# Moving one batch's chunk loads and two FFT insertions by a few steps in a filter-then-FFN kernel

## The chip, the cores and the metric

The kernel runs on one core of one Trainium2 chip. The metric is device time in microseconds (us). One execution can also be profiled; the profile is a page of summaries and a trace of all instructions. TensorE is PE in its lines, its weight loads PEld, VectorE DVE, ScalarE ACT, GpSimd POOL, and the queue of DMA issues on SyncE SPq.

## The reference

A spectral filter along the sequence, then a gated feed-forward network (FFN):

```python
X = np.fft.rfft(x, axis=1)                    # x: 8 x 3008 x 256, float32
y = np.fft.irfft(X * (filt_r + 1j*filt_i), n=3008, axis=1)
t = y.reshape(24064, 256)
out = (np.maximum(t @ w_gate, 0) * (t @ w_val)) @ w_out    # d_ff = 1536
```

## The kernel before

The FFN is the main loop: 47 blocks of 512 tokens, 12 steps each, so 564 steps. Step number n is block n // 12, ft n % 12. The FFT of later batches is cut in pieces that the loop puts between steps through a table of callbacks, `side`. Names used below: **psV, psG, psO** are the PSUM tiles of the FFN; **psF** is that of an excursion ("tiled A", the first DFT stage of a quarter batch); **dC** is a filtered spectrum read back from memory (Dbuf), which **psY** turns into **yT**, the FFN's input; **XP** is a chunk of x.

```python
def load_chunk(b, j):                 # six transfers, issued by GpSimd
    ...
def fold_chunk(b, j):                 # six adds on GpSimd, t from a pool of 2
    t = fs.tile([128, 2, 512], FP32, tag="fold", bufs=2, name="fold")
    tt(t, xp[:, 0:2], xp[:, 2:4], op=ALU.add)
    ...                               # cut: five more
def tiled_a(b, j):                    # the excursion
    banks = [ps.tile([128, 2, D], FP32, tag=t, name="psF") for t in ("psv", "psg", "fft", "fft")]
    ...                               # cut: 32 matmuls, then copies to asb (two on ScalarE, two on VectorE)

def hold_gpsimd(tile_):               # a tiny copy: GpSimd goes on when tile_ is written
    scr = sb.tile([128, 8], FP32, tag="scr", bufs=2)
    nc.gpsimd.tensor_copy(scr[:tile_.shape[0]], tile_)
...
C_AT = (8, 10)                        # the steps of a block at which psY is made (halves 0 and 1)
for b in range(1, B):
    end = (b * S // W - 1) * NFT + C_AT[0] - 5          # 123 for batch 2
    ...
        for j, e in enumerate((-74, -69, -64, -57)):
            l = (22, 34, 34, 46)[j] if b == 2 else end - 113 + NFT * j
            def next_x(b=b, j=j, l=l):
                hold_gpsimd(yTs[l // NFT + 1][:, 0, 0:8])
                load_chunk(b, j)
                if j: fold_chunk(b, j - 1)
                if j == 3: fold_chunk(b, j)
            at_step(l, next_x)
            at_step(end + e, lambda b=b, j=j: tiled_a(b, j))
...
for k in range(NB):
    for ft in range(NFT):
        gv(k, ft, prods)                                # psV, psG; ScalarE copies psV, VectorE makes prod
        if prev is not None: o_part(prev[0], ft, prev[1])   # four psO
        for f in side.get(k * NFT + ft, ()): f()        # FFT pieces
        if ft in C_AT and k + 1 < NB: item_c(k + 1, C_AT.index(ft))   # psY, then the copy to yT
```

Of the kernel before, what the change touches and what calls it, by code (L numbers as in the profile page):

```python
# [120 lines left out]
def kernel(  # L121
# [13 lines left out]
    NFT = DFF // 128  # L135
# [119 lines left out]
    def hold_gpsimd(tile_):  # L255

        scr = sb.tile([128, 8], FP32, tag="scr", bufs=2)
        nc.gpsimd.tensor_copy(scr[:tile_.shape[0]], tile_)  # L258
# [32 lines left out]
    def load_chunk(b, j):  # L291

        xp = XP[j]
        for q in range(4):
            r, o = 32 * q, 8 * q + 2 * j
            nc.gpsimd.dma_start(xp[r:r + 24, 0:4:2, :],  # L296
                              _ap(x, (b * N1 * N2 + o) * D,
                                  [[N2 * D, 24], [47 * N2 * D, 2], [1, 512]]))
        for i in range(2):
            nc.gpsimd.dma_start(xp[:, 2 * i + 1, :],  # L300
                              _ap(x, ((b * N1 + 46 + 47 * i) * N2 + 2 * j) * D,
                                  [[8 * D, 4], [-N2 * D, 32], [1, 512]]))

    def fold_chunk(b, j):

        xp = XP[j]
        t = fs.tile([128, 2, 512], FP32, tag="fold", bufs=2, name="fold")
        tt = nc.gpsimd.tensor_tensor
        tt(t, xp[:, 0:2], xp[:, 2:4], op=ALU.add)  # L309
        tt(xp[:, 2:4], xp[:, 0:2], xp[:, 2:4], op=ALU.subtract)  # L310
        tt(xp[:, 0], t[:, 0], t[:, 1], op=ALU.add)
        tt(t[:, 0], t[:, 0], t[:, 1], op=ALU.subtract)
        tt(t[:, 1], xp[:, 2], xp[:, 3], op=ALU.add)
        tt(xp[:, 2], xp[:, 2], xp[:, 3], op=ALU.subtract)
        fold[b, j] = (xp[:, 0], t[:, 0], t[:, 1], xp[:, 2])

    def tiled_a(b, j):

        banks = [ps.tile([128, 2, D], FP32, tag=t, name="psF") for t in ("psv", "psg", "fft", "fft")]
        for c in range(4):  # L320
            for q in range(4):
                r = 32 * q
                nc.tensor.matmul(banks[q][32 * c:32 * c + 32], WF[r:r + 24, c, :],  # L323
                                 fold[b, j][c][r:r + 24], start=True, stop=True,
                                 tile_position=(r, 32 * c))
        asf = sb.tile([128, NC2 * D], BF16, tag="asb", bufs=4, name="asb")
        asf = asf.rearrange("p (n q d) -> p n q d", n=2, d=D)
        for q in range(4):
            copy = nc.scalar.copy if q % 2 == 0 else nc.vector.tensor_copy
            copy(asf[:, :, q, :], banks[q])  # L330
        for c in range(4):
            nc.sync.dma_start(_ap(Abuf[b], ((48 * (c % 2) + 24 * (1 - c // 2)) * N2 + 8 * j) * D,
                                  [[N2 * D, 24], [1, 8 * D]]),
                              asf[32 * c:32 * c + 24])

    def load_at_tiled(b):

        ats[b] = sb.tile([128, NG, D], BF16, tag="at", bufs=1, name="at")
        for rr in range(4):
            nc.sync.dma_start(ats[b][32 * rr:32 * rr + 32],  # L340
                              _ap(Abuf[b], (48 * (rr % 2) + 24 * (rr // 2)) * N2 * D,
                                  [[D, 32], [N2 * D, 24], [1, D]]))
# [4 lines left out]
    def load_at(b, c):  # L347
        if c == 0:
            ats[b] = sb.tile([128, NG, D], BF16, tag="at", bufs=1, name="at")
        nc.sync.dma_start(ats[b][c:c + 125:4],  # L350
                          _ap(Abuf[b], c * NROW * NC2 * D, [[D, 32], [4 * NC2 * D, NG], [1, D]]))
# [4 lines left out]
    def fwd(b, i):  # L356

        for e in range(2):
            psXs[b, i, e] = ps.tile([128, 2, D], FP32, tag=fft_tag(), name="psX")
        for m in range(2):  # L360
            for e in range(2):
                for a in range(2):
                    j = 12 * a + 2 * i + m
                    nc.tensor.matmul(psXs[b, i, e][64 * a:64 * a + 64, m],  # L364
                                     F2[64 * e:64 * e + 64, j, :],
                                     ats[b][64 * e:64 * e + 64, j, :], start=True, stop=True,
                                     tile_position=(64 * e, 64 * a))

    def product(b, i, e, k, pool=False):

        psX = psXs[b, i, e]
        pool_, bufs = (fs, 4) if b else (pro, 6)
        p = pool_.tile([128, 2, D], BF16, tag=("tt", "uu")[k], bufs=bufs, name=("tt", "uu")[k])
        filt = (Ftr, Fti)[k][:, 4 * i + e:4 * i + 4:2, :]
        if pool:
            xs = pro.tile([128, 2, D], FP32, tag="xs", bufs=3)
            nc.scalar.copy(xs, psX)
            nc.gpsimd.tensor_tensor(p, xs, filt, op=ALU.mult)
        else:
            nc.vector.tensor_tensor(p, psX, filt, op=ALU.mult)  # L380
        tus[b, i, e, k] = p

    def inv(b, i, tags=None, cuts=CUTS):

        if i in cuts:
            dsbs[b] = i, sb.tile([128, 2, 4, D], BF16, tag="dsb", bufs=3, name="dsb")
        i0, dsb = dsbs[b]
        psD = [ps.tile([128, 2, D], FP32, tag=tags[a] if tags else fft_tag(), name="psD")
               for a in range(2)]
        for m in range(2):  # L390
            for k in range(2):
                for a in range(2):
                    for e in range(2):
                        nc.tensor.matmul(psD[a][64 * e:64 * e + 64, m],  # L394
                                         (I2t, I2u)[k][64 * a:64 * a + 64, 4 * i + 2 * m + e, :],
                                         tus[b, i, e, k][64 * a:64 * a + 64, m],
                                         start=(k == 0), stop=(k == 1),
                                         tile_position=(64 * a, 64 * e))
        o = 2 * (i - i0)
        for a in range(2):  # L400
            nc.scalar.copy(dsb[:, a, o:o + 2, :], psD[a])  # L401
        if i + 1 in cuts:
            nc.sync.dma_start(_ap(Dbuf[b], 2 * i0 * D, [[NG * D, 128], [NG // 2 * D, 2], [1, (o + 2) * D]]),
                              dsb[:, :, :o + 2, :])
# [18 lines left out]
    def load_d(b, z0=0, z1=NZ):  # L423
        for z in range(z0, z1):
            dC = sb.tile([NROW, 8, D], BF16, tag="dC", bufs=6)
            for e in range(2):
                nc.sync.dma_start(dC[48 * e:48 * e + 48],
                                  _ap(Dbuf[b], (64 * e + 16 * z) * NG * D,
                                      [[D, 48], [48 * D, 8], [1, D]]))
            dCs[b, z] = dC  # L430

    yTs = {}
# [177 lines left out]
    def at_step(s, f):  # L610
        side.setdefault(s, []).append(f)
# [5 lines left out]
    for b in range(1, B):  # L617
        end = (b * S // W - 1) * NFT + C_AT[0] - 5
        if b == 1:
            for c in range(2, 4):  # L620
                at_step(c - 2, lambda c=c: load_at(1, c))
        else:
            for j, e in enumerate((-74, -69, -64, -57)):
                l = (22, 34, 34, 46)[j] if b == 2 else end - 113 + NFT * j

                def next_x(b=b, j=j, l=l):
                    hold_gpsimd(yTs[l // NFT + 1][:, 0, 0:8])
                    load_chunk(b, j)
                    if j:
                        fold_chunk(b, j - 1)  # L630
                    if j == 3:
                        fold_chunk(b, j)
                at_step(l, next_x)
                at_step(end + e, lambda b=b, j=j: tiled_a(b, j))
            at_step(end + e + 4, lambda b=b: load_at_tiled(b))
        for i in range(7):
            l = -35 + 5 * i if b == 1 else -40 + 6 * i
            if i < 6:
                at_step(end + l, lambda b=b, i=i: fwd(b, i))
                for h in range(4):  # L640
                    at_step(end + l + h, lambda b=b, i=i, h=h: product(b, i, h // 2, h % 2))
            if i > 0:
                at_step(end + l, lambda b=b, i=i: inv(b, i - 1, ("psv", "psg")))
        at_step(end - 2, lambda b=b: load_d(b))
    prev = None
    for k in range(NB):
        prods = []
# [39 lines left out]
```

## Time and profile before

| | before |
|---|---|
| three runs known at the prediction | 899.38, 900.00, 900.28 us |
| the profiled run | 897.68 us, span 895.6 us |
| TensorE busy | 871.2 us, 97% |
| VectorE, ScalarE, GpSimd | 64%, 56%, 41% |
| mean granted clock | 0.999 |

TensorE is the bound, so a change pays by what it takes out of TensorE's own gaps. The prediction shows the gaps in batch 2. One more gap, in batch 5, in the timeline of TensorE (columns: start, duration, engine, line, operation, tiles, form, count; in brackets the idle time before and its releaser):

```profile
572.56 0.27 PE L451 MATMUL psY<-M,dC 96*128 96x4 bf16 x3
573.72 0.30 PE L451 MATMUL psY<-M,dC 96*128 96x94 bf16 x4 [0.89 <-DMA dC<-Dbuf]
```

The seven psY matmuls, normally in one go, are split: four waited for the data of dC.

### The profile page before, as it was taken

To read this page: it belongs to the slowest core of one execution; us is meant where nothing else is said; L and a number is where in the kernel's file an instruction comes from. 1 tells how busy PE (TensorE), PEld (TensorE's weight loads), DVE (VectorE), ACT (ScalarE), POOL (GpSimd) and SP (SyncE) were. 2 spreads that over 40 slices of the span, in tenths; PEclk is the share of its full clock that TensorE was granted. 3 is DMA by queue.
4 is the path that set the end of the run, shared out by engine and by line. 5 is a ranking of instruction groups with operands and counts; after the bars stand their busy time and mean duration, and the time that the engine had idled before them with its cause. 6 is when DMAs were issued, how large, how long until landed. Compare 5 with 4: busy or idle time off the path is not lost.

```text
span 895.6 us, 19081 instructions
## 1 busy us (share of the span) xinstructions
PE 871.2 (97%) x7086; PEld 507.4 (57%) x7206; DVE 569.3 (64%) x873; ACT 499.3 (56%) x891; POOL 364.4 (41%) x361
## 2 busy tenths in 40 slices
PE   7899999999999999999999999999999999999997
PEld 2335555566556665556655566556655556666665
DVE  2736865577665776667766676657766577655553
ACT  3475565556555556555655556555565555655553
POOL 4351399138661386415682167801868000000001
PEclk9999999999999999999999999999999999999999
DMA  8998358534466435563375333762346512231111
GB/s 240 284 241 166 110 143 181 123 81 113 128 156 132 112 106 133 136 141 95 100 174 135 97 99 106 180 134 85 110 143 150 119 31 82 74 81 36 37 32 52
DMA packets 114098, 109.17 MB, mean 122 GB/s; under 512 B 20359, under 2 KB 98599, under 8 KB 113366
## 3 DMA queue, kind: packets, MB, share of 16 engines
q1 hardware_dynamic: 90294, 80.10, 34.6%
q0 software_dynamic: 22992, 26.41, 12.4%
q8 instruction: 56, 0.92, 0.5%
q10 hardware_dynamic: 720, 1.45, 0.5%
q14 instruction: 36, 0.29, 0.1%
HBM read 61.93 MB, written 49.81 MB: 125 GB/s over the span
## 4 chain that ended last, share of the span: by engine, by line
PE 75%; POOL 6%; issue 5%; DVE 4%; DMA 4%; ACT 4%; SPq 0%; POOLq 0%; DVEq 0%; ACTq 0%
PE psG L467 23%; PE psO L486 22%; PE psV L467 21%; DVE prod L472 4%; ACT vsb L470 3%; PE psF L323 2%; PE psD L394 2%; PE psX L364 1%; DMA XP<-in_x_dram 1%; DMA Ftr<-in_filt_r_dram 1%; PE psY L451 1%; POOL XP L296 1%; DMA dC<-Dbuf 1%; POOL fold L309 1%; POOL XP L310 1%
## 5 line engine op out<-in xcount | busy, mean ns | idle before, releaser
L472 DVE SCALAR_TENSOR_TENSOR prod<-psG,vsb 128x512 bf16<-128x512 f32 x564 | 389.2, 690 | 263.5 <-ACT vsb L470 257.3
L470 ACT CAST vsb<-psV 128x512 bf16<-128x512 f32 x564 | 332.1, 589 | 261.3 <-PE psV L467 160.2
L486 PE MATMUL psO<-WoT,prod 128*128 128x256 bf16 x2256 | 336.4, 273 | 1.1
L467 PE MATMUL psG<-yT,WgT 128*128 128x512 bf16 x1107 | 330.8, 379 | 6.7 <-ACT dsb L401 0.6
L467 PE MATMUL psV<-yT,WvT 128*128 128x512 bf16 x1030 | 315.2, 380 | 0.3 <-ACT vsb L470 0.3
L486 PEld LDWEIGHTS <-prod 128*128 128x128 bf16 x2256 | 220.6, 98 | 143.4
L467 PEld LDWEIGHTS <-WgT 128*128 128x128 bf16 x1128 | 110.0, 98 | 135.8 <-issue 2.4
L467 PEld LDWEIGHTS <-WvT 128*128 128x128 bf16 x1128 | 98.4, 98 | 42.0 <-issue 30.8
L258 POOL CAST scr<-yT 128x8 f32<-128x8 bf16 x25 | 4.7, 189 | 262.2 <-ACT yT L456 262.2
L509 POOL DMA_DIRECT2D out_dram<-osb x5 | 2.6, 536 | 195.9 <-ACT osb L499 195.9
L380 DVE TENSOR_TENSOR tt<-psX,Ftr 128x512 bf16<-128x512 f32 x96 | 65.1, 683 | 7.1 <-PE psX L364 7.1
L499 ACT COPY osb<-psO 128x512 f32<-128x512 f32 x92 | 53.9, 586 | 27.4 <-PE psO L486 25.4
L309 POOL TENSOR_TENSOR fold<-XP 128x1024 f32<-128x1024 f32 x24 | 56.5, 2355 | 19.8 <-PE psF L323 19.6
L380 DVE TENSOR_TENSOR uu<-psX,Fti 128x512 bf16<-128x512 f32 x89 | 60.6, 681 | 0.0
L401 ACT CAST dsb<-psD 128x512 bf16<-128x512 f32 x96 | 51.5, 589 | 12.1 <-PE psD L394 11.7
L296 POOL DMA_DIRECT2D XP<-in_x_dram x96 | 56.7, 596 | 3.2 <-PE psG L467 1.6
L310 POOL TENSOR_TENSOR XP<-XP 128x1024 f32<-128x1024 f32 x24 | 56.3, 2348 | 1.9
L330 DVE CAST asb<-psF 128x512 bf16<-128x512 f32 x48 | 30.9, 686 | 20.9 <-PE psF L323 20.9
L330 ACT CAST asb<-psF 128x512 bf16<-128x512 f32 x48 | 25.8, 589 | 32.0 <-PE psF L323 32.0
L456 ACT CAST yT<-psY 128x512 bf16<-128x512 f32 x47 | 27.5, 586 | 26.0 <-PE psY L451 25.2
L451 PE MATMUL psY<-M,dC 96*128 96x94 bf16 (+18 forms) x604 | 37.7, 198 | 1.5 <-DMA dC<-Dbuf 1.4
L458 DVE CAST yT<-psY 128x512 bf16<-128x512 f32 x47 | 32.0, 681 | 9.8 <-PE psY L451 9.8
(69 smaller groups left out, 492.5 us busy)
## 6 DMA issues: line engine op xcount, KB each, us to landing
at<-Abuf SPq DMA_DIRECT2D x32, 384.0 KB
dC<-Dbuf SPq DMA_DIRECT2D x64, 192.0 KB
XP<-in_x_dram POOLq DMA_DIRECT2D x48, 256.0 KB, 6.1
Dbuf<-dsb SPq DMA_DIRECT2D x23, 512.0 KB
XP<-in_x_dram POOLq DMA_DIRECT2D x96, 96.0 KB, 2.6
Abuf<-asb SPq DMA_DIRECT2D x96, 96.0 KB
out_dram<-osb SPq DMA_DIRECT2D x69, 94.0 KB
XF<-in_x_dram SPq DMA_DIRECT2D x15, 256.0 KB
```

Source lines behind the costliest of these rows:

```text
L296: nc.gpsimd.dma_start(xp[r:r + 24, 0:4:2, :], _ap(x, (b * N1 * N2 + o) * D, [[N2 * D, 24], [47 * N2 * D, 2], [1, 512]]))
L309: tt(t, xp[:, 0:2], xp[:, 2:4], op=ALU.add)
L310: tt(xp[:, 2:4], xp[:, 0:2], xp[:, 2:4], op=ALU.subtract)
L330: copy(asf[:, :, q, :], banks[q])
L380: nc.vector.tensor_tensor(p, psX, filt, op=ALU.mult)
L401: nc.scalar.copy(dsb[:, a, o:o + 2, :], psD[a])
L451: nc.tensor.matmul(psY[:, o:o + w], dCs[b, n2 // 8][:, n2 % 8, h * 128:(h + 1) * 128], M1[:, n1:n1 + w], start=True, stop=True)
L467: nc.tensor.matmul(pt[:, :W], w[:, h, ft * 128:(ft + 1) * 128], yt[:, h, :], start=(h == 0), stop=(h == 1))
L470: nc.scalar.copy(vsb, psV[:, :W])
L472: nc.vector.scalar_tensor_tensor(prod, in0=psG[:, :W], scalar=0.0, in1=vsb, op0=ALU.max, op1=ALU.mult)
L486: nc.tensor.matmul(psO[:, t % 2], prods[ft][:, t * 128:(t + 1) * 128], WoT[:, ft, :], start=(ft == 0), stop=(ft == NFT - 1))
L499: copy(osb[:, t0 % 2:t % 2 + 1], psO[:, t0 % 2:t % 2 + 1])
```

## The change

Its intent: GpSimd finished folding two chunks of batch 2 after TensorE wanted them. So in batch 2 the second and the fourth chunk's loads get an earlier step, and the last two excursions a step two later. In batches 3 to 8 all loads get a step two earlier. In all of them the hold ahead of a load is put on the product of the step itself rather than on the next block's yT.

```diff
-            for j, e in enumerate((-74, -69, -64, -57)):
-                l = (22, 34, 34, 46)[j] if b == 2 else end - 113 + NFT * j
+            for j, e in enumerate((-74, -69, -62, -55) if b == 2 else (-74, -69, -64, -57)):
+                l = (22, 29, 34, 43)[j] if b == 2 else end - 115 + NFT * j
                 def next_x(b=b, j=j, l=l):
-                    hold_gpsimd(yTs[l // NFT + 1][:, 0, 0:8])
+                    hold_gpsimd(prods[-1][:, 0:8])
```

## The prediction

> **What bounds the kernel now.** The first table of the page gives TensorE 871.2 us busy of a span of 895.6 us, 97%; VectorE has 64%, ScalarE 56%, GpSimd 41%. The chain that ended last is 75% TensorE. So only what stops TensorE can be worth anything, and the question is where it stops.
>
> The main loop has 47 blocks of 12 steps, 564 in all. One step is two psV matmuls, two psG, then four psO; a batch's FFT work is put between steps. A "tiled A excursion" (psF, 32 matmuls) is such an insertion: it reads a chunk of x that GpSimd has loaded and folded with six additions. I read the timeline of TensorE next, by the starts. A bare step runs from one psV to the next in 1.30 us (153.18, 154.48, 155.78). In batch 2 the loop puts the four excursions at steps 49, 54, 59 and 66 (end is 123; minus 74, 69, 64, 57), which are the psF starts at 130.99, 138.66, 146.83 and 158.47:
>
> ```profile
> 137.27 0.59 PE L467 MATMUL psV<-yT,WvT 128*128 128x512 bf16 x2
> ...
> 138.66 0.63 PE L323 MATMUL psF<-XP,WF 24*32 24x512 f32 x4
> ...
> 139.74 0.39 PE L467 MATMUL psV<-yT,WvT 128*128 128x512 bf16 x1
> ...
> 145.41 0.60 PE L467 MATMUL psV<-yT,WvT 128*128 128x512 bf16 x2
> ...
> 146.83 0.63 PE L323 MATMUL psF<-XP,WF 24*32 24x512 f32 x4
> ...
> 148.28 1.06 PE L323 MATMUL psF<-XP,WF 24*32 24x512 f32 x8 [0.29 <-POOL XP L314]
> 149.27 0.39 PE L467 MATMUL psV<-yT,WvT 128*128 128x512 bf16 x1
> ...
> 157.08 0.59 PE L467 MATMUL psV<-yT,WvT 128*128 128x512 bf16 x2
> ...
> 159.89 1.06 PE L323 MATMUL psF<-XP,WF 24*32 24x512 f32 x8 [0.28 <-POOL XP L314]
> 160.88 0.60 PE L467 MATMUL psV<-yT,WvT 128*128 128x512 bf16 x2
> ```
>
> The reader is to measure psV to psV across each. The second excursion takes 139.74 - 137.27 = 2.47 us, so a ready excursion costs 2.47 - 1.30 = 1.17. The third takes 149.27 - 145.41 = 3.86 and the fourth 160.88 - 157.08 = 3.80. They lose **1.39 and 1.33 us, 2.72 us together**. The bracket says only 0.29 and 0.28, because modelled ends of earlier matmuls cover most of the gap. The releaser is GpSimd's last fold addition, so I read its timeline:
>
> ```profile
> 105.67 0.19 POOL L258 CAST scr<-yT 128x8 f32<-128x8 bf16 x1 [15.01 <-ACT yT L456]
> ...
> 120.10 0.19 POOL L258 CAST scr<-yT 128x8 f32<-128x8 bf16 x1
> ...
> 134.13 0.19 POOL L258 CAST scr<-yT 128x8 f32<-128x8 bf16 x1
> ...
> 146.95 1.27 POOL L314 TENSOR_TENSOR XP<-XP 128x512 f32<-128x512 f32 x1
> 149.68 2.35 POOL L309 TENSOR_TENSOR fold<-XP 128x1024 f32<-128x1024 f32 x1 [1.46 <-PE psF L323]
> ...
> 158.57 1.27 POOL L314 TENSOR_TENSOR XP<-XP 128x512 f32<-128x512 f32 x1
> ```
>
> GpSimd sat idle until 105.67 (the hold on y) and was then busy without a gap until 148.2: the third fold ends there, after its excursion has begun, and the fourth ends at 159.84. The page names psF for the 1.46 us before 149.68, but the fold buffer needed there had been free since the second excursion (139.7). The chain of waits shows instead "137.32 12.12 DMA XP<-in_x_dram", that is, the fourth chunk landed at 149.44. So the queue started too late, and the last chunk landed late. In batch 3 all four excursions take 2.46 or 2.47 us: no other batch has anything to win here.
>
> **What the Trainium skill says.** "Perfetto Trace Analysis", section "Per-engine timelines", has a matmul's recorded end computed, not observed. The trace agrees: records of one step add to 0.59 + 0.59 + 0.60 = 1.78 us where starts are 1.30 apart. Hence I use starts. "GPSIMD Engine Reference", section 3.1, has a 2048-element fp32 add at 4497 ns; half of that is 2249, and the 1024-element adds here take 2355, so a fold is not shortened by moving it. "SBUF — State Buffer", section "Who interferes with whom", lets GpSimd and VectorE collide only where VectorE uses the shared ports, not with a single SBUF input. The product has one (the other is in PSUM), and it takes 0.69 us both at 150.95 beside a fold and at 165.10 with GpSimd idle: folds may move freely beside it. "DMA: Bandwidth & Descriptors", section "Issuing engines are not separate DMA queues", says that all transfers interleave on the same 16 engines; the 12.12 us of the fourth chunk beside the batch's dC load agree (the median landing over all XP issues is 2.7).
>
> **The change part by part.** No instruction is added or removed (the order of the two programs has the same rows on every engine). Three things move.
>
> *1. Batch 2's chunks.* Loads at steps 22, 34, 34, 46 become 22, 29, 34, 43, and the hold is on the product of that very step. Before, the holds were on y of the next block, made at ft 8, so steps 20, 32, 32, 44 set them free. From the trace: six load issues take 3.8 us (120.2 to 124.0), one fold 10.1 (124.0 to 134.1). Step 29's psV is near 98.4 (psV 103.23 is step 32, 2.18 before it step 31, two steps of 1.30 before that), its product ends near 100.4. Then GpSimd goes: loads 100.6 to 104.5, fold 1 to 114.6, loads to 118.5, fold 2 to 128.6, loads to 132.5, fold 3 (its buffer comes free with the first excursion, 132.3) to 142.5, fold 4 to 152.6. These are estimates from those durations: 5.6 us sooner for fold 3. If the fourth chunk again takes 12 us it lands near 144.5 and fold 4 ends near 154.6.
>
> *2. Two excursions two steps later.* The third moves to step 61, at 146.83 + 2 x 1.30 = 149.4, some 7 us after its fold. The fourth moves to 68, at 158.47 - 1.39 + 2.60 = 159.7, 5 to 7 us after its fold. Both waits go: **-2.72 us**. Either movement alone would nearly do (5.6 us sooner, or 2.6 later against 1.4 needed).
>
> *3. A new neighbour.* Step 68 is ft 8, where the next y is made straight after the excursion, with psY in the same pair of psv buffers. psV of step 68, psF, psY and psV of step 69 take turns in two buffers, so psV of step 69 must wait for ScalarE's copy of psF. At ft 1, 6 and 11 there is no psY and that copy is hidden. The copy starts 1.30 us after psF (132.29 against 130.99) and takes 0.59, and psV can start at about 1.94; without the wait it would at 1.07 + 0.27 (psY at 163.50, psV at 163.76) = 1.34. **+0.60 us.** There is a precedent in batch 1, an inverse transform followed by psY in one step:
>
> ```profile
> 126.24 0.41 PE L451 MATMUL psY<-M,dC 96*128 96x20 bf16 x7
> 126.50 0.38 PE L467 MATMUL psV<-yT,WvT 128*128 128x512 bf16 x1
> 127.43 0.59 PE L467 MATMUL psG<-yT,WgT 128*128 128x512 bf16 x2 [0.56 <-ACT dsb L401]
> ```
>
> *4. Batches 3 to 8.* Loads go from ft 10 to ft 8, but the old hold was already set free by ScalarE's y at ft 8: at 180.75 in batch 3, where the product of the same step ends at 180.27 (179.57 + 0.70). So they start only about 0.45 us sooner, and their folds 3 and 4 still wait for psF. The one loss there is in batch 5, where dC arrived late (a wait of 0.9 us at 573.7, after a Dbuf write that shared the DMA engines with a chunk). It may shrink: I put -0.1.
>
> Sum: -2.72 + 0.60 - 0.1 = **-2.2 us**, so 900.0 - 2.2 = 897.8.
>
> **The rivals.** (a) *The whole 2.7 us is won or more*: ScalarE's copy is hidden after all and the dC wait goes, 896.4. Against it is the precedent above. (b) *A new transfer wait takes over*: the fourth chunk is now issued at 128.6 to 132.5, on top of the Dbuf write of 127.4, for which the dC load waits (132.48), and dC is needed at 142.34. For it: the DMA share is 0.86 in 130 to 140. Against it: the same bytes competed before, two or three microseconds later. If dC were 1 to 2 us late, the time is 899 to 900. (c) *Reading batch 2's A back becomes late*: its load moves from step 70 to 72, behind five output writes, near 169 to 171 us; it took until about 174 from 165.3, and its reader at step 83 is near 182. Some 4 us remain; if not, about 899. (d) *GpSimd is still too slow*, if additions slow down or the chunk lands later: 7 us of slack speak against it; 900.
>
> **Range and chances.** The total at stake is 2.7 us of 900, 0.3%, so a move of over 2% (18 us) would need something the profile gives no sign of. The middle is 897.8. Half the known terms gone wrong give 899.4, everything right with a little more gives 896.2, and run-to-run spread is about 0.5 us. Chances: faster 0.005, within 2% 0.985, slower 0.01.
>
> **What would show it.** In the changed profile psV to psV across the third excursion should be 2.47 us instead of 3.86, and across the fourth 1.30 + 1.17 + 0.27 + 0.60 = 3.34, with the wait on psV naming ScalarE's asb. GpSimd's folds in batch 2 should end near 114, 128, 142 and 153, and no psF should name GpSimd beyond 0.2 us. In batch 3 the first hold should end about 0.45 us sooner against its step. The prediction is wrong if dC or at waits appear near 142 or 182, or if step 69's psV doesn't wait.

## The result, and the profile after

The changed kernel took 895.93 us (median of 4 runs, 894.64 to 896.87). Before, the three known runs and one more, took 899.69 us (898.14 to 900.28). The ratio is 0.996, interval 0.9942 to 0.9978. The time is 0.27 us below the low end of the predicted range (896.2).

In batch 2 the two traces differ where expected. First TensorE's timeline after, around the third and fourth excursion:

```profile
150.62 0.63 PE L323 MATMUL psF<-XP,WF 24*32 24x512 f32 x4
...
151.69 0.60 PE L467 MATMUL psV<-yT,WvT 128*128 128x512 bf16 x2
...
160.89 0.63 PE L323 MATMUL psF<-XP,WF 24*32 24x512 f32 x4
...
161.97 0.42 PE L451 MATMUL psY<-M,dC 96*128 96x30 bf16 x7
162.83 0.59 PE L467 MATMUL psV<-yT,WvT 128*128 128x512 bf16 x2 [0.45 <-ACT asb L330]
```

No psF has GpSimd in a bracket any more. The excursion is 1.07 us from psF to psV, where the third took 2.44 before. The fourth is now followed by psY, and psV of step 69 waits for ScalarE's copy of psF (asb). Then GpSimd's timeline after:

```profile
101.81 0.19 POOL L258 CAST scr<-prod 128x8 f32<-128x8 bf16 x1 [6.23 <-DVE prod L472]
...
143.09 1.27 POOL L314 TENSOR_TENSOR XP<-XP 128x512 f32<-128x512 f32 x1
145.52 2.35 POOL L309 TENSOR_TENSOR fold<-XP 128x1024 f32<-128x1024 f32 x1 [1.16 <-DMA XP<-in_x_dram]
...
154.43 1.26 POOL L314 TENSOR_TENSOR XP<-XP 128x512 f32<-128x512 f32 x1
```

Fold 3 ends at 144.4 for a psF at 150.6, fold 4 at 155.7 for one at 160.9. And in batch 5 the psY is whole:

```profile
572.09 0.42 PE L451 MATMUL psY<-M,dC 96*128 96x4 bf16 x7
```

To take the two traces apart I used the start of the first psO matmul of every step, which is there for all steps from 12 on, and which no modelled end can blur. Starts are printed to 0.01 us, so a difference is good to about 0.01. "Step 59 took 3.85" means from its first psO to that of step 60. After minus before, accumulated: the changed kernel begins step 12 **1.00 us late**, where the two programs have not yet differed in anything. By step 59 it is 1.19 late. Step 59 then gives 2.55, step 61 costs 1.17, step 66 gives 2.51, step 68 costs 1.77: net 2.12 us. Later, gaps of 0.23 us each appear at steps 286 and 334 (a weight load with the label "issue"; I didn't find out more), and step 344, that of the late dC, gives 1.05. From the start of step 12 to that of step 563 the loop took 808.65 us instead of 811.17, 2.52 less. But from there to the end of the span the changed kernel took 11.50 us instead of 10.52, 0.98 more, and with the 1.00 of the start the spans differ by 0.5 only, and the times of these two runs, 896.87 and 897.68, by 0.8. So the profiled pair doesn't contain the 3.8 us of the medians at all, and a part of that may not be the change's.

### The profile page after: what moved, and what is told of

The parts are those of the page before. It is cut to its first block, busy times and chain, and to the rows that moved or that the text cites. A ratio compares the mean times of both kernels' runs of the same rounds, so it can differ in the third digit from the quotient of the medians.

```text
span 895.1 us, 19152 instructions
## 1 busy us (share of the span) xinstructions
PE 878.4 (98%) x7206; PEld 507.2 (57%) x7206; DVE 569.2 (64%) x873; ACT 498.8 (56%) x891; POOL 364.4 (41%) x361
## 4 chain that ended last, share of the span: by engine, by line
PE 94%; DMA 2%; ACT 1%; POOL 1%; SPq 1%; DVE 1%; issue 1%; ACTq 0%; POOLq 0%
PE psV L467 28%; PE psG L467 27%; PE psO L486 27%; PE psF L323 3%; PE psD L394 2%; PE psY L451 2%; PE psX L364 2%; PE psA L276 1%; DMA XF<-in_x_dram 1%; PE psJ L520 1%; SPq L176 1%; DVE prod L472 0%; ACT dsb L401 0%; DMA dC<-Dbuf 0%; POOL out_dram L509 0%
## 5 line engine op out<-in xcount | busy, mean ns | idle before, releaser
L467 PE MATMUL psV<-yT,WvT 128*128 128x512 bf16 x1128 | 336.6, 380 | 0.8 <-ACT asb L330 0.5
L467 PE MATMUL psG<-yT,WgT 128*128 128x512 bf16 x1128 | 335.5, 379 | 0.9 <-ACT dsb L401 0.3
L258 POOL CAST scr<-prod 128x8 f32<-128x8 bf16 x24 | 4.5, 189 | 257.7 <-DVE prod L472 257.7
```

The source lines that it names most:

```text
L467: nc.tensor.matmul(pt[:, :W], w[:, h, ft * 128:(ft + 1) * 128], yt[:, h, :], start=(h == 0), stop=(h == 1))
```

## The experiments

**Theory M**: the mechanism and its size are as predicted, -2.72 + 0.60 in batch 2 and a little in batch 5. **Rival R**: the later batches' earlier holds give 1.5 us more. **Rival C**: the first comparison, four runs against four, was off because runs of one kernel differ by more than I had taken. Each run below was compared with the kernel before on the same chip; all differences are far under 2%, so it is their size that is asked for. Diffs are against the changed kernel unless said otherwise, and written without conditions whose branches are equal.

**The changed kernel again** (no edit).

> The changed kernel once more, unaltered, for a better sized difference. Theory M (only batch 2's two waits, less the new psV wait, is what changed): ratio near 0.9976, 2.2 us. Rival R (the later batches add about 1.5 us through dC waits that come and go): 0.996 again, 3.6 us. Rival C (the first comparison was the spread of a few runs): a ratio between 0.996 and 0.9985 with runs of one kernel 1 to 2 us apart.

Measured: 897.05 us median (894.56 to 899.11), before 897.91 (896.18 to 901.19, 11 runs), ratio 0.9982, interval 0.996 to 1.0004. Single runs of one kernel are 4.5 and 5.0 us apart: Rival C. In its trace a new wait shows, which the first one did not have:

```profile
144.87 0.36 PE L451 MATMUL psY<-M,dC 96*128 96x72 bf16 x5
146.58 0.20 PE L451 MATMUL psY<-M,dC 96*128 96x64 bf16 x1 [1.35 <-DMA dC<-Dbuf]
146.62 0.60 PE L467 MATMUL psV<-yT,WvT 128*128 128x512 bf16 x2
```

This is batch 1's dC at step 56, late by 1.5 us (3.05 instead of 1.53): rival (b) of the prediction, in one run of the same kernel and not in another.

**Batch 2 alone**: its new steps and hold; later batches as before.

```diff
-                l = (22, 29, 34, 43)[j] if b == 2 else end - 115 + NFT * j
+                l = (22, 29, 34, 43)[j] if b == 2 else end - 113 + NFT * j
-                    hold_gpsimd(prods[-1][:, 0:8])
+                    hold_gpsimd(prods[-1][:, 0:8] if b == 2 else yTs[l // NFT + 1][:, 0, 0:8])
```

> Batch 2's steps and hold as changed, batches 3 to 8 as before. Theory M: as the whole change, ratio 0.9976, and in the trace -2.55, +1.17, -2.51, +1.77 us at steps 60, 62, 67, 69. Rival R: only 2.1 of the 3.6 us come, ratio 0.9977 where the whole change has 0.996, and the dC wait of about 1 us near step 345 stays.

Measured: 896.57 us (895.76 to 898.51), ratio 0.9985 (0.9967 to 1.0002). Steps 59, 61, 66, 68 took 1.30, 2.48, 1.30, 3.33 us, the same as in the whole change; step 344 took 1.89, a wait of 0.33. The times can't separate M from R; the trace has M's steps.

**The later batches alone**: the mirror image, batch 2 as before.

```diff
-            for j, e in enumerate((-74, -69, -62, -55) if b == 2 else (-74, -69, -64, -57)):
-                l = (22, 29, 34, 43)[j] if b == 2 else end - 115 + NFT * j
+            for j, e in enumerate((-74, -69, -64, -57)):
+                l = (22, 34, 34, 46)[j] if b == 2 else end - 115 + NFT * j
-                    hold_gpsimd(prods[-1][:, 0:8])
+                    hold_gpsimd(yTs[l // NFT + 1][:, 0, 0:8] if b == 2 else prods[-1][:, 0:8])
```

> Batches 3 to 8 as changed (two steps earlier, held by the product), batch 2 as before. Theory M: same as before within 0.3 us, ratio 0.9997 to 1.0. Rival R: 1 to 1.5 us faster, ratio 0.9985, and no psY waits for dC in the trace. The two psF waits on GpSimd in batch 2 stay at 1.3 to 1.4 us.

Measured: 897.76 us (897.31 to 899.23), ratio 0.9999 (0.9982 to 1.0015). The loop took 811.08 us, 0.09 less than in the first trace of before, and step 344 still took 2.47. Rival R falls by the trace: this part alone gives nothing that can be seen there (the interval of the times alone would still hold R's 0.9985). On top of batch 2's part it gives nothing either: the loop took 808.89 us without it, 808.65 and 809.00 with it where dC was in time.

**The new loads, excursions at their old steps.**

```diff
-            for j, e in enumerate((-74, -69, -62, -55) if b == 2 else (-74, -69, -64, -57)):
+            for j, e in enumerate((-74, -69, -64, -57)):
```

> As changed, but batch 2's last two excursions back at their old steps 59 and 66, so no psY follows an excursion. Theory M: both GpSimd waits are gone by the earlier folds alone (fold 3 ends near 144.4 for a psF at 147.9, fold 4 near 155.7 for one at 157.2), and the 0.5 to 0.6 us wait of psV of step 69 is gone too: 0.6 us faster than the whole change, ratio near 0.9970 where the whole change has 0.9976. If the later steps were needed, psF at step 66 waits for GpSimd and the time is that of the whole change or more.

Measured: 895.34 us (894.06 to 895.94), ratio 0.9967 (0.995 to 0.9983), the best of the four. TensorE at the third and fourth excursion:

```profile
148.31 0.63 PE L323 MATMUL psF<-XP,WF 24*32 24x512 f32 x4
...
149.38 0.60 PE L467 MATMUL psV<-yT,WvT 128*128 128x512 bf16 x2
...
158.58 0.63 PE L323 MATMUL psF<-XP,WF 24*32 24x512 f32 x4
...
159.66 0.60 PE L467 MATMUL psV<-yT,WvT 128*128 128x512 bf16 x2
```

Both are 1.07 to 1.08 us from psF to psV, without a bracket. The earlier loads suffice, and the later steps only add the wait behind psY: this trace's steps 12 to 72 took 93.51 us, against 94.22 in the changed kernel's first trace and 96.15 before.

**The kernel before against itself** (no edit).

> The kernel before, unaltered, against itself: this sizes the spread. Theory C (start of the program and late dC loads vary from run to run by 1 to 3 us, whatever the kernel): ratio within 0.998 to 1.002 of 1 and single runs 2 to 4 us apart; in its trace the loop from step 12 to 563 takes 810 to 811.2 us as in the first trace of before, with losses of 2.55 and 2.51 us at steps 59 and 66 over a bare step, while the time at which step 12 begins differs by 1 us or more from 73.93. Rival R would have runs of one kernel within 0.5 us and the change's 3.6 us intact.

Measured: 898.63 us (896.78 to 901.45), against 899.61 (897.19 to 901.09) for the same program: ratio 0.9997 (0.9977 to 1.0018). Six runs against eleven leave an interval of 0.2% to either side, nearly as large as the whole effect. Its loop took 811.50 us, a little above what was expected, and its step 12 began at 74.98. Its fourth excursion was worse than in the first trace:

```profile
159.57 0.63 PE L323 MATMUL psF<-XP,WF 24*32 24x512 f32 x4
...
161.64 1.06 PE L323 MATMUL psF<-XP,WF 24*32 24x512 f32 x8 [0.28 <-POOL XP L314]
162.64 0.60 PE L467 MATMUL psV<-yT,WvT 128*128 128x512 bf16 x2
```

From psF to psV it is 3.07 us, 2.0 over a ready one, where the first trace had lost 1.34. The bracket says 0.28 both times.

**The changed kernel a third time** (no edit).

> The changed kernel, unaltered, a third time. Theory M and C: ratio 0.9976, within 0.996 to 0.999; pooled with the two earlier ones 2.0 to 2.7 us; in the trace batch 2's part from step 12 to 73 is 94.2 us against 96.15 of before, unless dC is late at step 56 as in the second run (95.87).

Measured: 896.02 us (895.07 to 896.84), ratio 0.9968 (0.9952 to 0.9983). Steps 12 to 72 took 94.56 us, the loop 809.00; the 0.34 us over the first trace all lie at step 16, before any of the changed steps.

**The new loads with old excursion steps again** (no edit).

> Earlier loads with the excursions at their old steps, unaltered, again. Theory M: 0.6 us faster than the changed kernel, ratio near 0.9970; steps 12 to 73 in 93.5 us, no psV waits for asb. If the 0.9967 of the last time was luck: the ratio is that of the changed kernel or worse.

Measured: 895.31 us (893.92 to 896.67), ratio 0.9959 (0.9943 to 0.9975). Steps 12 to 72 took 93.51 us again.

**Two loads five steps sooner still**, to have the fourth chunk out of the way of Dbuf and dC. The base is the kernel with old excursion steps.

```diff
-                l = (22, 29, 34, 43)[j] if b == 2 else end - 115 + NFT * j
+                l = (22, 24, 29, 38)[j] if b == 2 else end - 115 + NFT * j
```

> As the one before, but batch 2's second and fourth chunk loads five steps sooner still (steps 22, 24, 29, 38), so that the fourth chunk is issued near 124 to 128 us, ahead of the Dbuf write and of batch 1's dC load, in place of beside them. Theory that the fourth chunk is what makes dC late at step 56: dC is never late there, and steps 12 to 73 take 93.5 us. Rival: lateness there has another source, and a wait can still show. Time as the one before, ratio 0.997 or 0.3 us better.

Measured: 896.41 us (894.98 to 896.91), ratio 0.997 (0.9955 to 0.9986). This missed its aim: with two chunks under way at once, fold 1 waited 6.76 us for its chunk, so the fourth chunk's issue moved not earlier but 0.6 us later relative to step 49. dC was late at step 56, 3.01 us. It says nothing against the theory and shows that an earlier step is not an earlier transfer.

**The later excursions alone**: batch 2's loads and hold as before.

```diff
-                l = (22, 29, 34, 43)[j] if b == 2 else end - 115 + NFT * j
+                l = (22, 34, 34, 46)[j] if b == 2 else end - 115 + NFT * j
-                    hold_gpsimd(prods[-1][:, 0:8])
+                    hold_gpsimd(yTs[l // NFT + 1][:, 0, 0:8] if b == 2 else prods[-1][:, 0:8])
```

> Batch 2's last two excursions two steps later, its loads and hold as before (later batches as changed). Theory M: fold 3 still ends near 148.2 and fold 4 near 159.8, but psF now comes at 149.4 and near 159.7, so both waits are gone or under 0.2 us by the later steps alone; the wait of 0.5 to 0.6 us of psV of step 69 is there; ratio 0.9976 like the whole change. If the fourth chunk lands late, as once in a trace of before (fold 4 0.6 us later), psF at step 68 waits up to 0.7 us: the loads are what gives the margin.

Measured: 896.11 us (895.52 to 897.86), before 897.86 (895.92 to 900.58, 11 runs), ratio 0.9982 (0.9966 to 0.9997). Step 61 took 2.48, so the third wait is gone by the later step alone. Step 68 took 3.62 instead of 3.33: fold 4 ended at 159.73, and a wait of 0.3 us for it remains. So either half of batch 2's change removes nearly all of the 2.7 us.

**The fourth chunk loaded straight after the third**, ahead of the second fold, in the kernel with old excursion steps.

```diff
-                    load_chunk(b, j)
+                    if b != 2 or j < 3:
+                        load_chunk(b, j)
+                    if b == 2 and j == 2:
+                        load_chunk(b, 3)
                     if j:
                         fold_chunk(b, j - 1)
```

> As the earlier loads with the excursions at their old steps, but the fourth chunk is loaded straight after the third, ahead of fold 2, so near 120 to 124 us, before the Dbuf write (128.5) and the dC load (132). An earlier try to do this by earlier steps alone did not move that load. Theory that the fourth chunk beside the dC load is what makes dC late at step 56 in 2 of 7 traces with the new loads: no wait there in this one, fold 4 waits for no transfer, steps 12 to 73 in 93.5 us, ratio 0.996 to 0.997 with a narrow spread. Rival (lateness comes from elsewhere): waits at step 56 still show in a part of the traces.

> The same kernel once more, for a second trace and more times: as the one before, ratio 0.996 to 0.997; step 56 in 1.53 us if the theory holds.

Measured: 894.98 us (894.21 to 897.32), ratio 0.9968 (0.995 to 0.9986), and 895.15 us (893.78 to 896.16), ratio 0.9966 (0.995 to 0.9982). This time the load did move, to 120.2 us, ahead of the fold:

```profile
120.19 2.33 POOL L296 DMA_DIRECT2D XP<-in_x_dram  x4
122.52 1.40 POOL L300 DMA_DIRECT2D XP<-in_x_dram  x2
123.93 2.36 POOL L309 TENSOR_TENSOR fold<-XP 128x1024 f32<-128x1024 f32 x1
...
144.33 2.35 POOL L309 TENSOR_TENSOR fold<-XP 128x1024 f32<-128x1024 f32 x1
```

Fold 4, at 144.33, now has no wait for a transfer. Step 56 took 1.54 and 1.53 us, and the loops took 807.94 us both times. That fits the theory, but the two traces of the kernel it builds on had no late dC either (loops 807.95 and 807.94), so two clean traces don't prove it. What the traces do show is that the fourth chunk draws dC's load out. dC is loaded by eight transfers issued one after the other; from the first of these issues to the last it took 3.47 and 3.45 us here, but 6.11 to 10.79 us in the seven traces that have the new loads and the chunk beside dC (3.55 to 4.49 in the four with the old loads, where the chunk comes behind dC's first issues). Of the two late ones one has the longest, 10.79, but the other 6.65, no more than punctual ones. So the step from drawn out to late stays argued.

All traces by their steps (us, to within 0.01; a ready step 56 is 1.53, a ready excursion step 2.47, a bare step 1.30; step 344 is 1.56 when dC is in time):

| kernel | step 12 begins | 56 | 59 | 61 | 66 | 68 | 344 | steps 12 to 563 |
|---|---|---|---|---|---|---|---|---|
| before | 73.93 | 1.53 | 3.85 | 1.31 | 3.82 | 1.56 | 2.61 | 811.17 |
| before, again | 74.98 | 1.54 | 3.88 | 1.30 | 4.47 | 1.56 | 2.23 | 811.50 |
| later batches alone | 75.58 | 1.53 | 3.81 | 1.30 | 3.87 | 1.56 | 2.47 | 811.08 |
| later excursions alone | 73.48 | 1.53 | 1.30 | 2.48 | 1.30 | 3.62 | 2.88 | 809.63 |
| changed | 74.93 | 1.53 | 1.30 | 2.47 | 1.30 | 3.33 | 1.56 | 808.65 |
| changed, again | 76.20 | 3.05 | 1.30 | 2.47 | 1.30 | 3.33 | 1.56 | 810.30 |
| changed, third | 75.14 | 1.53 | 1.30 | 2.48 | 1.30 | 3.33 | 1.56 | 809.00 |
| batch 2 alone | 77.15 | 1.53 | 1.30 | 2.48 | 1.30 | 3.33 | 1.89 | 808.89 |
| new loads, old excursions | 75.34 | 1.53 | 2.47 | 1.30 | 2.48 | 1.56 | 1.56 | 807.95 |
| the same, again | 76.11 | 1.53 | 2.47 | 1.31 | 2.48 | 1.56 | 1.56 | 807.94 |
| two loads sooner still | 74.64 | 3.01 | 2.48 | 1.30 | 2.48 | 1.56 | 1.56 | 809.36 |
| fourth chunk ahead | 75.11 | 1.54 | 2.48 | 1.30 | 2.48 | 1.56 | 1.56 | 807.94 |
| the same, again | 74.89 | 1.53 | 2.47 | 1.31 | 2.48 | 1.56 | 1.56 | 807.94 |

The column of step 12 is the point for Rival C. All thirteen programs are the same up to there, and it begins between 73.48 and 77.15 us. The loop of one kernel repeats to 0.1 us, but for late transfers and up to 0.34 us at step 16; the start does not.

The traces say more about the start. From its first psY matmul to step 12 it takes 15.29 to 15.38 us in all thirteen, so the spread lies before that. The first psX matmul (the DFT stage that reads the first stage's result back) comes at 35.22 to 37.48 us. From there to the last psX of the start it takes 11.63 us in four traces and 12.09 to 13.84 in nine, and the granted TensorE clock between 40 and 45 us (in the lines below the third number from the end) is 1.00 in exactly these four and 0.50 to 0.68 in the nine. Two of them, the first traces of before and of the changed kernel:

```profile
40.00:45.00 5.00, 4.28 (x62) 1.81 (x55) 2.72 (x5) 4.49 (x9) 4.59 (x5) 1.00 1.08 345
40.00:45.00 5.00, 4.69 (x39) 1.85 (x38) 2.69 (x5) 3.80 (x8) 4.74 (x5) 0.66 1.05 329
```

The mean clock over the span, 0.999 and 0.998, hides this. It goes with up to 2.2 us of the start; what delays the first psX by up to 2.3 us, and what lowers the clock, I didn't trace. The end varies too: from the start of step 563 it takes 10.35 to 10.55 us in ten traces, 10.95, 11.41 and 11.50 in three.

## Why the prediction was wrong

*The step that failed is the range*, in these words: "run-to-run spread is about 0.5 us", and with it the starting point "900.0". The mechanism in batch 2 was right; of the terms of the sum only batch 5's -0.1 was mis-sized (below). Three runs within 0.9 us had made the spread look small. They were not typical: over all comparisons the kernel before was timed 43 times, from 895.92 to 901.45, mean 898.55, standard deviation 1.5 us. The sign was there beforehand: the profiled run, 897.68 us, was 1.7 below the lowest of the three, and I left it out. In the three comparisons that hold both kernels, 32 runs of before average 898.70 and 16 of the changed kernel 896.32: a difference of **2.4 us**, with a standard error of 0.43 (from deviations of 1.52 and 1.32). The forecast was 2.2. Of the 1.87 us between the forecast 897.8 and the measured 895.93, then, 1.30 is the starting point (900.0 against 898.70), 0.39 the draw of these four runs (895.93 against 896.32) and only 0.18 the change itself. The single comparisons gave ratios of 0.996, 0.9982 and 0.9968, that is 3.6, 1.6 and 2.9 us (plain means of all runs: 3.6, 1.0 and 3.0). So the first one's 3.6 was the largest draw of three; three of its four runs of before were the known ones, and the one new run, 898.14, is 2.3 above the changed kernel's mean, for what a single run is worth. That this excess is mostly the start and the end of the program is likely, not shown: only profiled runs tell where their time went. With 1.5 us a run, medians of three and of four runs differ by chance by some 1.25 x 1.5 x sqrt(1/3 + 1/4) = 1.4 us, so an 8 in 10 range from that alone is 897.8 plus or minus 1.8; with the doubt about the mechanism on top it should have been about 895.5 to 900 (an estimate with hindsight: the 1.5 was measured later).

*Each step of the mechanism:*

- Both GpSimd waits, -2.72: right. Steps 59 and 66 lost 1.38 and 1.34 us over ready ones in the first trace (3.85 and 3.82 against 2.47 and 2.48), and nothing of that is left. The fourth varies, up to 2.0.
- The new neighbour, +0.60: right. Step 68 took 3.33, and 3.33 - 1.56 - 1.17 is 0.60; the wait names asb as foretold. It falls away with the old excursion steps, where step 68 takes 1.56.
- Fold ends near 114, 128, 142 and 153: they were 116.3, 130.3, 144.4 and 155.7. The first three are 1.7 to 1.9 us later than the working had it (114.6, 128.6, 142.5), of which 1.2 is this run's late start and more than half of the rest the idle 0.38 us between the hold and the first load issue, which the working left out (it stands in the trace of before too, ahead of 106.24); the fourth waited 1.16 more for its transfer.
- Later batches 0.45 us sooner: right, but worth little. The hold came 1.14 us after step 80's first psO instead of 1.57.
- Batch 5, -0.1: too small. Step 344 gives 0.7 to 1.05, less the two gaps of 0.23, which stand in the same eight traces (that of batch 2 alone has such gaps at steps 190 and 238 instead). That wait is absent in all eight traces with both new loads and new later holds, and there in all four with batch 2's old loads. With the new loads and the old later holds it is 0.33 us. Neither part alone removes it. In the eight traces dC's load is first issued 4.5 to 5.1 us before step 344's first psO, in the other five 3.5 to 4.2; why batch 2's loads matter so far downstream stays open.
- Rival (b), batch 1's dC late: real, not steady. It cost 1.5 us in one of the three traces of the changed kernel. It showed in two of the nine traces in which batch 2's loads had been moved and in none of the four in which they had not. That the fourth chunk draws dC's load out is shown, that this makes it late is argued. (The prediction's median landing of 2.7 us mixes transfers of 96 and 256 KB; for those of 256 KB, like the one of 12.12 us, it was 6.1.)
- Rival (c), the A read-back: nothing. No wait for it shows in any of the traces.
- Rival (a), "the whole 2.7 us is won": false for the change, true for the kernel with old excursion steps. Its 12 runs average 895.22, 1.1 below the changed kernel's 16 (standard error 0.40); its loop is 0.7 us shorter than the changed kernel's best. With the fourth chunk ahead 12 runs average 895.11, on a chip for which no run of the changed kernel is recorded. Both versions' averages are below those of both kernels.

## What to carry to other kernels

When TensorE is busy 97% of the time, measure a wait from start to start against the same piece of work where it is ready; the idle time that the profile puts in a bracket can be a fifth of it. Of two remedies, an earlier producer and a later consumer, try each alone: here either was nearly enough, and the later consumer met a new neighbour that took back 0.6 us. Before giving a range narrower than 1%, time the unchanged kernel more than three times, compare loops from trace to trace, and keep the part of the program that did not change out of the comparison. A mean clock of 0.999 doesn't mean full clock in every stage: look at the short ones by themselves.

## What the Trainium skill lacked or had wrong

- "Perfetto Trace Analysis", section "Per-engine timelines", rightly has matmul ends as estimates. It lacks what follows for idle times: a bracket of 0.29 us stood for a loss of 1.37 (2.44 from psF to psV against 1.07), and one of 0.28 for both 1.34 and 2.0.
- "DMA: Bandwidth & Descriptors", section "Anatomy of one DMA — SWDGE (gpsimd) path", fits one transfer by 2.0 us plus its bytes over 436e3 per us. For the 256 KB pieces of a chunk that is an estimate of 2.6 us. The median landing over the whole trace of before was 6.1 us (each is issued right behind other transfers of its chunk), and the fourth chunk of batch 2 took 12.12 us beside the dC load. A fit for a transfer that shares the engines is missing.
- "GPSIMD Engine Reference", section 3.1: its 4497 ns for a 2048-element add agrees. Adds of 1024 and 512 elements took 2356 and 1267 ns, so 1089 per 512 elements and 178 fixed, which makes 4534 for 2048 (an estimate). The page has no figure in ns for the fixed part of GpSimd, and half of its number (2249 ns, an estimate) was 4.5% short of the 2356.
- None of the pages that I read says how far runs of one kernel on one core differ. Here 43 runs, over several chips, spread over 5.5 us (0.6%), and the start of the program alone over 3.7 us in thirteen traces.
